# A three-stage kernel (linear attention, mixture of experts, SoLU layer): the last stage's blocks all behind the expert pairs

## The chip, the cores and the metric

One core of a Trainium2 chip runs the whole program in one launch. The metric is the device time of one execution in microseconds (us). Engines are named as in the profile: PE (TensorE, matmul), PEld (its weight loads), DVE (VectorE), ACT (ScalarE), POOL (GpSimd), SP (SyncE, which here only reads registers and issues DMAs).

## What is computed

The reference, cut to what matters (8 batches, 8 heads, 576 positions, so 4608 tokens of 512 numbers; 8 experts; inner width 1024):

```
proj = x @ w_phi ; proj -= max|proj| ; phi = [exp(proj), exp(-proj)]      # for q and k
num = phi(q) @ (phi(k)^T v) ; den = phi(q) @ sum phi(k) ; x = num / den
logits = x @ w_gate + modality_bias[modality] ; e = argmax ; gate = softmax(logits)[e]
y = gate * (relu(x @ w1[e]) @ w2[e])                                       # one expert per token
h = y @ w_in ; solu = h * softmax(h) ; out = (layernorm(solu) * g_ln) @ w_out
```

All matrix products that matter are done as three products of a high part and a low part (`mm3`, line 1071): high by high, high by low, low by high. So each operand has to be split first: ACT copies the high part (rounded), and DVE or POOL subtracts it from the source to get the low part.

## The kernel before

**Stage 1, attention and gating** (lines 194 to 732) scatters each token's row into a list per expert in DRAM (`xe`). On its heels DVE works out a small table (`slot_table`, lines 735 to 833): which expert, which rows and which output columns each "unit" of the next stage has. SP reads its registers from that table, and nothing of the next stage that depends on them can be loaded before.

**Stage 2, the experts** (`moe`, from line 955). Units 0 and 1 belong to the fullest expert, which is known early; their weights are loaded and split before the table is there. Units 2 to 17 are pairs (256 tokens), unit 18 is a single (128 tokens), then four minis of up to 32 tokens are done together in `quad` (line 1317). A unit is two products: `mm1` (line 1114) with four weight chunks, `mm2` (line 1169) with four more. `split_raw` (line 928) splits one chunk of 128x1024: high part on ACT, low part on DVE, or on POOL where line 933 says so: for unit 1 the chunks in `POOL_FIRST`, which is (1, 3); for units from `NOPOOL` = 13 on the chunks in `POOL_SPLIT`, also (3, 7). `used` (line 1063) is called as each chunk has been multiplied: it splits the chunk `LOOK` = 4 ahead, has SP reload the raw buffer for the next unit (for the minis after unit 18: `load_mini`), and advances the preparation `bg`.

**The preparation** (`weights`, lines 974 to 1021) loads, converts and splits the last stage's weights `win` and `wout` in 65 small steps, mostly on DVE. `NPREP` (line 1054) spreads them evenly over the chunks of the units before `START`.

**Stage 3, the last stage**, is done in 36 blocks of 128 tokens. `load_y` fetches two blocks' `y` from DRAM, `yT` splits it (ACT, then POOL), `a3` (line 1223) multiplies by `win` into `h` (24 matmuls) and runs a chain on DVE and ACT (maxima, exponent, scaling) that ends in the tile `ex`; `lnT` (line 1248) transposes `ex` on PE and splits it; `a4` (line 1262) multiplies by `wout` (24 matmuls) and POOL scatters the rows to the output. One call of `block` (line 1427) issues, in this order: `lnT(i)`, any postponed transposes of an expert unit (`run_mids`), `yT(i+2)`, the load for a later pair of blocks, `a3(i+1)`, `a4(i)`. The first call has only `yT(1)` and `a3(0)`.

**Where the blocks stand.** `unit` (line 1381) calls `gap` ahead of `mm1` and between `mm1` and `mm2`; from unit `START` = 14 on, `gap` runs a block. Ahead of unit `START` - 1 `load_y(0)` is issued, behind it `yT(0)`. In `quad`, one block follows each step. What blocks are then left run by themselves. The single unit keeps its hidden rows in `m.hr`: two Relu (line 1142) write it, and `tr_single` (line 1102), postponed with `run_mids`, transposes and splits it before `mm2`. The single's output is likewise copied off PSUM (`yr`, line 1157) and transposed later (line 1162).

**The order of the instructions.** Inside `manual_schedule` the engines named take their instructions in the order in which the program issues them; elsewhere a planner orders them by its own simulation. Units 2 to 12 (up to `NMAN`) are issued with PE, ACT, DVE, POOL and SP all in program order, units 13 to 18 with SP alone; `quad` with PE, and the blocks after it with all.

```
def units(u0, u1):
    for u in range(u0, u1):
        if u == START - 1: run(bg); load_y(0)
        unit(u)
        if u == START - 1: yT(0)
with tc.manual_schedule(engines=MANUAL): units(2, NMAN)
units(NMAN, NU)                                   # NU = 19
with tc.manual_schedule(engines=QMAN):
    for _ in quad(): block()
while state[0] < NT: block()
```

Of the kernel before, what the change touches and what calls it, by code (L numbers as in the profile page):

```python
# [25 lines left out]
NPAIR = 16  # L26
NSING = 1
# [20 lines left out]
RING = 5  # L48
RING0 = 1
STEP0 = 6  # L50
POOL_FIRST = (1, 3)
LOOK = 4
MANUAL = {mybir.EngineType.PE, mybir.EngineType.Activation, mybir.EngineType.DVE, mybir.EngineType.Pool}

# [805 lines left out]
class Moe:  # L860
# [67 lines left out]
    def split_raw(self, s, i):  # L928
# [3 lines left out]
        lo = pool.tile([P, DFF], F32R, name=nm[1])  # L932
        pe = POOL_FIRST if s == 1 and i < 4 else POOL_EARLY if s < NOPOOL else POOL_SPLIT
        self.split(self.raw[i], hi, lo, self.tc.nc.gpsimd if i in pe else self.tc.nc.vector)
# [20 lines left out]
def moe(ctx, m):  # L955
# [97 lines left out]
    NSTEP = 4 * (2 * KD + KF) + 2  # L1053
    NPREP = 8 * (START - 2) - 6

    def split_to(j):
        while done[0] <= min(j, len(order) - 1):
            ch = order[done[0]]
            done[0] += 1
            m.split_raw(*ch)  # L1060
            reload(*ch)

    def used(ch):
        split_to(pos[ch] + LOOK)
        if 2 <= ch[0] < START:
            uses[0] += 1
# [150 lines left out]
    def yT(i):  # L1217
        hi = p2.tile([P, KD, P], F32R, name="yTh")
        lo = p2.tile([P, KD, P], F32R, name="yTl")
        m.split(ys[i][0], hi, lo, G)  # L1220
        yt[i] = (hi, lo)
# [146 lines left out]
    def run(g):  # L1368
        for _ in g:
            pass  # L1370
# [10 lines left out]
    def unit(u):  # L1381
        gap(u)
        g = mm1(u)
        for i in range(4):
            next(g)
            if i == XAT:
                run_mids()
                next_x(u)
        run(g)
        gap(u)  # L1390
        run_mids()
        run(mm2([u]))
# [34 lines left out]
    def block():  # L1427
        i = state[0]
        state[0] += 1
        if 0 <= i < NT:  # L1430
            lnT(i)
        run_mids()
        if i + 2 < NT:
            yT(i + 2)
            if i % 2 and i + 3 < NT:
                load_y((i + 3) // 2)
        if i + 1 < NT:
            a3(i + 1)
        if 0 <= i < NT:
            a4(i)  # L1440

    def gap(u):
        if u >= START:
            block()

    def units(u0, u1):
        for u in range(u0, u1):
            if u == START - 1:
                run(bg)
                load_y(0)  # L1450
            unit(u)
            if u == START - 1:
                yT(0)

    with tc.manual_schedule(engines=MANUAL):
        units(2, NMAN)
    units(NMAN, NU)
    if ENDMAN:
# [7 lines left out]

XAT = 1
ENDMAN = True
START = 14
NMAN = START - 1  # L1470
QMAN = {mybir.EngineType.PE}
NOPOOL = 13


POOL_SPLIT = (3, 7)
# [57 lines left out]
```

## Time and profile before

| | before |
|---|---|
| median of 3 runs | 1337.44 us (1335.55 to 1338.93) |
| the profiled execution's own time | 1330.52 us |
| its span (first to last instruction) | 1328.8 us |
| mean granted clock of PE | 0.995 |
| busy: PE, PEld, DVE, ACT, POOL | 98%, 82%, 61%, 50%, 33% of the span |
| DMA | 120 MB by the queues, mean 90 GB/s |

Busy time is a share of the whole span; it says nothing of which engine the end waits for at a given moment. That is read from the waits and from the chain that ended last. PE's clock is given as a share of full speed (1.00 is 2.4 GHz, 0.50 is 1.2 GHz); a stretch with a value between spent part of it at either.

### The profile page before, as it was taken

The numbers are of one execution on the slowest core, as the hardware profiler recorded it, in microseconds if no ns is written. First come the engines' busy times: TensorE is split into PE (matmuls) and PEld (weight loads), VectorE is DVE, ScalarE is ACT, GpSimd is POOL, SyncE is SP. The second block draws the span as 40 slices with busy tenths as digits, with TensorE's granted clock in tenths as the row PEclk, the third lists the DMA queues.
The fourth block names the chain that finished last, engine by engine and source line by source line (L and its number), as shares of the span: only waits on it lengthen the run. The fifth ranks groups of instructions, "written<-read, shape, count | busy, mean of one in ns | idle before, by whom it ended". The sixth has DMA issues, their size and how long they took to land.

```text
span 1328.8 us, 25500 instructions
## 1 busy us (share of the span) xinstructions
PE 1298.4 (98%) x9522; PEld 1092.2 (82%) x9522; DVE 811.5 (61%) x1571; ACT 668.1 (50%) x1254; POOL 433.8 (33%) x493
## 2 busy tenths in 40 slices
PE   8999999999999989999999999999999999999997
PEld 7677777777775889999999999898987777888885
DVE  8758867866885748888888654444433334444442
ACT  6666666666664345555565554444433333443332
POOL 7555665674672200000000322232312232322331
PEclk9999999999999989999999999999999999999998
DMA  8712421341142132224432211124435542111110
GB/s 239 208 52 63 133 94 56 98 136 49 50 134 76 67 95 80 74 71 142 145 80 81 65 41 56 41 61 146 127 81 159 159 145 70 49 40 48 40 41 24
DMA packets 123119, 120.08 MB, mean 90 GB/s; under 512 B 35664, under 2 KB 109552, under 8 KB 122992
## 3 DMA queue, kind: packets, MB, share of 16 engines
q1 hardware_dynamic: 117008, 99.30, 25.6%
q0 software_dynamic: 5824, 19.04, 3.9%
q8 instruction: 77, 1.26, 0.4%
q14 instruction: 50, 0.41, 0.1%
q10 hardware_dynamic: 160, 0.07, 0.0%
HBM read 148.32 MB, written 33.02 MB: 136 GB/s over the span
## 4 chain that ended last, share of the span: by engine, by line
PE 63%; issue 1%; ACT 0%; POOL 0%; POOLq 0%
PE tp L1074 43%; PE h L1074 15%; PE tp L1098 2%; PE tp L898 1%; PE tp L1349 1%; PE tp L1333 1%; PE tp L1280 0%; POOLq L1529 0%; ACT sq L1253 0%; ACT lnTh L887 0%; PE tp L1109 0%; ACT wab L1268 0%; POOL rs L1258 0%; PE tp L1162 0%; POOL rs L1256 0%
## 5 line engine op out<-in xcount | busy, mean ns | idle before, releaser
L322 POOL TENSOR_TENSOR es<-es,e 128x512 f32<-128x512 f32 x128 | 163.6, 1285 | 103.9 <-ACT e L278 92.3
L1074 PE MATMUL tp<-xTh,whi 128*128 128x256 f32 x432 | 122.5, 284 | 2.9 <-PEq L1412 2.9
L1233 DVE TENSOR_REDUCE s_mx<-h 128x1 f32<-128x512 f32 x72 | 46.4, 686 | 125.4 <-PE h L1074 125.4
L1074 PE MATMUL tp<-xTh,wlo 128*128 128x256 f32 x432 | 121.5, 281 | 1.2 <-DVE wlo L926 1.2
L1074 PE MATMUL tp<-xTl,whi 128*128 128x256 f32 x432 | 121.3, 281 | 0.0
L1074 PE MATMUL tp<-hTl,whi 128*128 128x256 f32 x432 | 120.9, 280 | 0.0
L1074 PE MATMUL tp<-hTh,wlo 128*128 128x256 f32 x432 | 120.8, 280 | 0.0
L1074 PE MATMUL tp<-hTh,whi 128*128 128x256 f32 x432 | 120.7, 280 | 0.0
L926 POOL TENSOR_TENSOR wlo<-ldk,whi 128x1024 fp32r<-128x1024 f32 x6 | 14.6, 2435 | 314.8 <-PE tp L1074 296.0
L1269 POOL DMA_INDIRECT out_dram<-wab,gt x36 | 38.5, 1070 | 222.5 <-ACT wab L1268 221.8
L1238 ACT ACTIVATE ex<-h,s_mx,gt 128x1024 f32<-128x1024 f32 x36 | 43.4, 1206 | 134.2 <-DVE s_mx L1235 70.6
L271 DVE TENSOR_REDUCE m<-mm 128x4 f32<-128x512 f32 x144 | 97.1, 680 | 16.0 <-PE mm L269 15.9
L259 DVE TENSOR_TENSOR lo<-tp,hi 128x512 fp32r<-128x512 f32 x72 | 49.5, 688 | 84.0 <-ACT hi L258 83.5
L267 PE MATMUL mm<-wphi_hi,hi 128*128 128x256 f32 x288 | 93.5, 325 | 1.0 <-ACT hi L258 1.0
L1074 PEld LDWEIGHTS tp<-xTh,whi 128*128 128x128 f32 x432 | 82.0, 190 | 3.3 <-issue 3.1
L888 DVE TENSOR_TENSOR lnTl<-tp,lnTh 128x512 fp32r<-128x512 f32 x74 | 47.6, 685 | 58.4 <-ACT lnTh L887 58.4
L1074 PEld LDWEIGHTS tp<-xTh,wlo 128*128 128x128 f32 x432 | 82.0, 190 | 1.5 <-DVE wlo L926 1.5
L338 ACT ACTIVATE qp<-tp 128x512 f32<-128x512 f32 x128 | 69.4, 597 | 26.1 <-PE tp L330 23.2
L1074 PEld LDWEIGHTS tp<-xTl,whi 128*128 128x128 f32 x432 | 82.0, 190 | 0.2
L1074 PEld LDWEIGHTS tp<-hTh,whi 128*128 128x128 f32 x432 | 81.5, 189 | 0.4
L1074 PEld LDWEIGHTS tp<-hTl,whi 128*128 128x128 f32 x432 | 81.5, 189 | 0.3 <-DVE hTl L1089 0.2
L1074 PEld LDWEIGHTS tp<-hTh,wlo 128*128 128x128 f32 x432 | 81.5, 189 | 0.2
(427 smaller groups left out, 3928.2 us busy)
## 6 DMA issues: line engine op xcount, KB each, us to landing
ldk<-in_moe_w_dram SPq DMA_DIRECT2D x66, 512.0 KB
ldv<-in_moe_w_dram SPq DMA_DIRECT2D x66, 512.0 KB
ldq<-in_moe_w_dram SPq DMA_DIRECT2D x44, 512.0 KB
yd<-yo SPq DMA_DIRECT2D x36, 256.0 KB
yin<-yd SPq DMA_DIRECT2D x18, 512.0 KB
xin<-xe SPq DMA_DIRECT2D x16, 512.0 KB
ldk<-in_k_dram SPq DMA_DIRECT2D x15, 512.0 KB
ldq<-in_q_dram SPq DMA_DIRECT2D x15, 512.0 KB
```

The costliest lines, as they stand in the source:

```text
L259: V.tensor_tensor(out=lo, in0=tp, in1=hi.bitcast(F32), op=ALU.subtract)
L267: T.matmul(o, lhsT=hi[:, 2 * a + j, :], rhs=c.wphi_hi, start=(j == 0), stop=False, skip_group_check=True)
L271: V.tensor_reduce(out=m, in_=pj, axis=AX.X, op=ALU.max, apply_absolute_value=True)
L322: G.tensor_tensor(out=eo, in0=eo, in1=ev[:, :, r, :], op=ALU.add)
L338: A.activation(u.qp[half][:, fh, 2 * hp : 2 * hp + 2, o : o + 2 * P], tp.rearrange("p (h r) t -> p h (r t)", r=2), AF.Exp, scale=sc,)
L888: self.tc.nc.vector.tensor_tensor(out=lo, in0=tp, in1=hi.bitcast(F32), op=ALU.subtract)
L926: eng.tensor_tensor(out=lo, in0=src, in1=hi.bitcast(F32), op=ALU.subtract)
L1074: T.matmul(o, lhsT=l, rhs=r, start=first and n == 0, stop=last and n == 2, skip_group_check=True)
L1098: T.transpose(tp[:, j, :], src[:, (b0 + j) * P : (b0 + j + 1) * P], c.ident)
L1233: V.tensor_reduce(out=mx, in_=h[:, sl], axis=AX.X, op=ALU.max, negate=True)
L1238: A.activation(ex, h, AF.Exp, bias=mx, scale=g, accum_out=sm)
L1269: ins = G.indirect_dma_start(out=out, out_offset=bass.IndirectOffsetOnAxis(ap=ys.pop(i)[2].bitcast(I32), axis=0), in_=ob, in_offset=None,)
```

## The change

Five constants change, nothing else. `START` becomes 2 + 16 + 1 = 19, one behind the last unit. So `gap` never runs a block; `load_y(0)` moves from ahead of unit 13 to ahead of unit 18 and `yT(0)` from behind unit 13 to behind unit 18; the ten blocks that ran in units 14 to 18 join those in and behind `quad`. The preparation is spread over the chunks of units 2 to 18 instead of 2 to 13 (`NPREP` is 130 instead of 90). `NMAN` becomes 19: units 13 to 18 are now issued in program order on all engines. `POOL_FIRST` is empty and `NOPOOL` is 19, so no low part of an expert weight is on POOL any more: 2 of unit 1 and 12 of units 13 to 18 move to DVE.

```diff
-POOL_FIRST = (1, 3)
+POOL_FIRST = ()
...
-START = 14
-NMAN = START - 1
+START = 2 + NPAIR + NSING
+NMAN = START
 QMAN = {mybir.EngineType.PE}
-NOPOOL = 13
+NOPOOL = START
```

## Rows read from the trace of the kernel before

**Rows 1.** The profile's page: busy time, share of the span and instructions of each engine.

```profile
PE 1298.4 (98%) x9522; PEld 1092.2 (82%) x9522; DVE 811.5 (61%) x1571; ACT 668.1 (50%) x1254; POOL 433.8 (33%) x493
```

**Rows 2.** Busy time by stretch: length, engines (instructions), PE clock, DMA share, GB/s.

```profile
438.00:478.00 40.00, 32.59 (x259) 31.94 (x259) 27.68 (x98) 15.83 (x22) 5.74 (x3) 0.96 0.13 37
478.00:743.00 265.00, 265.00 (x2251) 264.84 (x2250) 218.55 (x298) 143.09 (x196) 2.63 (x1) 0.99 0.33 96
743.00:993.00 250.00, 250.00 (x1643) 227.01 (x1642) 115.90 (x183) 113.15 (x170) 72.46 (x72) 1.00 0.27 79
993.00:1131.00 138.00, 138.00 (x831) 106.56 (x830) 52.86 (x110) 48.37 (x86) 36.77 (x60) 1.00 0.41 130
1131.00:1309.50 178.50, 178.50 (x833) 145.43 (x831) 76.85 (x159) 67.92 (x121) 53.95 (x89) 1.00 0.14 42
```

**Rows 3.** The chain that ended last: start us, us, engine, tile, line, count.

```profile
696.92 22.49 PE tp L1074 x192
...
743.72 16.88 PE tp L1074 x144
...
1288.04 0.87 PE tp L1098 x8
1288.91 5.59 PE h L1074 x24
```

**Rows 4.** PE's waits from 438 us to the end: total us, times, longest.

```profile
PE tp L898 <- DMA xin<-xe: 3.0, 1, 3.0
PE tp L1074 <- PEq L1412: 2.9, 1, 2.9
PE tp L1074 <- DVE wlo L926: 1.2, 1, 1.2
```

**Rows 5.** Timeline around the table: start us, us, engine, line [idle before].

```profile
438.47 5.47 DVE L751 TENSOR_TENSOR st_tail<-st_tail,st_mini 128x8 f32<-128x8 f32 x1
...
439.12 2.44 POOL L926 TENSOR_TENSOR wlo<-ldq,whi 128x1024 fp32r<-128x1024 f32 x1
...
441.50 2.40 POOL L926 TENSOR_TENSOR wlo<-ldk,whi 128x1024 fp32r<-128x1024 f32 x1
...
444.00 0.15 DVE L751 TENSOR_TENSOR st_num<-st_all,st_tail 128x8 f32<-128x8 f32 x1
...
459.70 0.17 DVE L832 CAST st_tab<-st_res 128x5 int32<-128x5 f32 x1
...
462.46 0.39 SPq L913 DMA_DIRECT2D xin<-xe  x1
...
467.60 1.06 PE L898 MATMUL tp<-ident,xin 128*128 128x128 f32 x8 [2.96 <-DMA xin<-xe]
```

**Rows 6.** Busy time by stretch behind PE's three waits, columns as in the second group.

```profile
446.00:465.00 19.00, 18.43 (x154) 18.22 (x154) 13.70 (x75) 3.38 (x5) 0.00 (x0) 1.00 0.07 18
465.00:472.00 7.00, 4.40 (x25) 4.43 (x26) 4.18 (x5) 4.98 (x7) 0.00 (x0) 0.76 0.10 30
...
478.00:485.00 7.00, 7.00 (x49) 7.00 (x48) 0.69 (x1) 1.36 (x2) 0.00 (x0) 0.76 0.71 143
```

**Rows 7.** Groups by form, 478 to 1000 us (POOL: 743 to 1310): busy us, mean ns.

```profile
L1142 ACT ACTIVATE ldq<-tp 128x512 f32<-128x512 f32 x2 | 1.2, 592 | 0.1
L925 ACT CAST whi<-ldk 128x1024 fp32r<-128x1024 f32 x40 | 42.4, 1060 | 16.0 <-PE tp L1074 9.5 <-issue 4.0 <-DMA ldq<-in_moe_w_dram 1.7
L925 ACT CAST yTh<-yin 128x512 fp32r<-128x512 f32 x13 | 8.0, 623 | 40.6 <-DMA yin<-yd 28.7 <-PE h L1074 11.8
...
L926 DVE TENSOR_TENSOR wlo<-ldk,whi 128x1024 fp32r<-128x1024 f32 x35 | 43.6, 1246 | 12.6 <-ACT whi L925 12.3
L888 DVE TENSOR_TENSOR xTl<-tp,xTh 128x512 fp32r<-128x512 f32 x31 | 20.0, 685 | 17.0 <-ACT xTh L887 17.0
...
L926 POOL TENSOR_TENSOR yTl<-yin,yTh 128x512 fp32r<-128x512 f32 x36 | 47.4, 1318 | 65.8 <-ACT yTh L925 65.8
```

**Rows 8.** DVE timeline of one late block: first and last step of its chain.

```profile
1294.54 1.29 DVE L1233 TENSOR_REDUCE s_mx<-h 128x1 f32<-128x512 f32 x2 [3.93 <-PE h L1074]
...
1299.21 0.88 DVE L1245 TENSOR_SCALAR ex<-ex,s_tot 128x512 f32<-128x512 f32 x2
```

## The prediction

> **What bounds the kernel now.** I read the page first, then the busy time by stretch, the chain that ended last, PE's waits, and last the timeline where those waits are. The page says PE is busy for 98% of the span [rows 1]; the stretches say where the rest is not. From 478 to 1309.5 us PE is busy for every microsecond, in the pairs alone, in the pairs mixed with blocks, in the minis and in the blocks alone [rows 2]. The chain that ended last is PE from end to end there. Its pace tells whether a busy PE hides slack: 192 matmuls of a pair alone in 22.49 us are 117 ns each, 144 between blocks in 16.88 us also 117 ns, and 24 matmuls of a block, twice as wide, in 5.59 us are 233 ns [rows 3]. So a matmul costs the same wherever it stands, and moving ten blocks moves PE work without making it smaller. What can change is idle time of PE: three waits at the start of the experts, of 1.2, 3.0 and 2.9 us [rows 4], and any that the new order makes. DVE, ACT and POOL have room everywhere in these stretches [rows 2].
>
> **What goes away, at the front.** POOL's two low parts of unit 1 run from 439.12 to 443.90. Across both of them DVE is held in one tiny subtraction of the table for 5.47 us, though the like of it takes 0.15 [rows 5]: 5.3 us lost. From there DVE is busy without a pause up to the table's last step at 459.70, SP then issues the load of `xin` at 462.46, and PE stands 2.96 us until that has landed [rows 5]. With the change DVE does the two low parts itself, 2 x 1.25 = 2.5 us by the group of its low parts [rows 7], and is not held. The table, and all behind it, comes 5.3 - 2.5 = **2.8 us** earlier. PE's 1.2 us wait for a low part of POOL's [rows 4] goes, so PE reaches the transposes of `xin` 1.2 us earlier and waits about 1.4 us instead of 3.0; the sum is the same 2.8. The wait of 1.2 us left the clock at 1.00; after the waits of 3.0 and 2.9 us it was 0.76 over 7 us each time, which is 0.24 x 7 = 1.7 us lost per wait [rows 6]. I take it that the shortened wait no longer costs that: **1.7 us**. The wait at the branch (2.9, line 1412) stays: PE's own sequencer is what it waits for. Front: -4.5. Bounds: at best all of 1.2 + 3.0 + 1.7 = 5.9; at worst nothing, if the planner, which still orders the table, puts the two low parts ahead of more of it.
>
> The Trainium skill ("SBUF — State Buffer", "Who interferes with whom") has DVE with two SBUF inputs and a reading GpSimd instruction exclude each other, for the whole of the instruction that came first. The row agrees that DVE stands still, but it stood for two POOL instructions, not one; by the page's one, what goes would be 2.4 us, about as much as DVE takes on. That case is among the rivals.
>
> **What is moved at no cost.** Twelve low parts of units 13 to 18 come to DVE, 1.25 us each [rows 7], two per unit. In the pairs alone DVE already does all eight of a unit and the whole preparation in eleven units, 218.55 us of 265, and PE never waits [rows 2]; spread over sixteen units the preparation weighs less. If that cover were gone, PE would wait at a chunk, at most 1.25 us each. `load_y(0)` now stands in SP's queue between the last output writes of unit 17 and the chunk reloads and mini weights of unit 18, and waits for those writes as it did for unit 12's; a load of that size landed 5.1 us after issue [rows 5], and unit 18 takes 11 us. A moved block takes its loads, its split on POOL and its scatter along; the blocks alone need 53.95 us of POOL in 178.5 [rows 2].
>
> **What the new order adds.** PE now has nothing between the steps at the seam of experts and blocks. Three holes, priced by the rows of the pieces:
> - In unit 18 a block used to stand between `mm1` and `mm2`. Now, after the last matmul of `mm1`: Relu 0.59, the high part of the last chunk 1.06 (ahead on ACT in program order), its low part 1.25 on DVE, then the low part of the first hidden half 0.69: 3.6 us to the first matmul that needs it [rows 7]. PE fills 0.87 with eight transposes [rows 3] and 0.2 with two matmuls. Hole: **2.5**. Bounds 0.8 (Relu, copy and low part without the chunk) to 3.6 (nothing filled).
> - After unit 18 the single's rows are copied off PSUM, about 0.6 like the Relu, and transposed, 0.44; `yT(0)` behind it needs 0.62 on ACT and 1.3 on POOL [rows 7] before the third matmul of `a3(0)`. 0.6 + 0.62 + 1.3 and some 0.4 for starts are 2.9, of which PE fills 0.9. Hole: **2.0**, bounds 0.6 to 2.6.
> - The first block's chain: from the end of `h` to a whole `ex` it is 1294.54 to 1300.09, 5.55 us [rows 8]. In the steady run `a4` of the block before, 5.59 us [rows 3], just covers it. For block 0 there is no such `a4`, and in program order only the four transposes of the minis' input, 0.44 us, stand between; the transposes of `ex` can start some 0.3 before its end. Hole: **4.8**, bounds 4.8 to 5.2. Before, unit 14's `mm1` of 11 us filled it.
> - A hole longer than the 2.9 us that was followed by a 0.76 clock should cost 1.7 us again [rows 6]; the two shorter, broken holes I take like the 1.2 us that cost nothing. **1.7**, bounds 0 to 3.4.
>
> Seam: +11.0, bounds 6.2 to 14.8. **Sum:** -4.5 + 11.0 = +6.5 us. The profiled execution would go from 1328.8 to 1335.3 us of span, 1337.0 with the 1.7 around it. It lies 6.9 us under the median of the runs shown, so the sum is put on the median: 1337.4 + 6.5 = **1343.9 us**, slower by 0.5%. A measurement of this kernel can tell about 0.3%, 4.0 us, from no change. The ends give +0.3 to +14.8.
>
> **The rivals.**
> - Nearly even: the front gives its full 5.9 and the two short holes stay near their lower bounds. +0.3 to +4 us, some 1340. For it: both short holes are sums of single steps in program order, some of which may overlap. Against: the 4.8 alone nearly eats the 5.9.
> - Faster: the seam is covered, since PE's order is not as written (a planner that slips the single unit's or the minis' matmuls ahead of the waiting transposes). Then only the front is left, 1337.4 - 4.5 = 1332.9. It decides if under 0.5 us of holes is left. Against: the change puts PE in program order through units 13 to 18, `quad` and the blocks, and the late blocks of the chain come out exactly as issued [rows 3].
> - The lock is short: one POOL instruction's worth. The table comes no earlier, PE's 1.2 us only moves into the wait for `xin`, and the front gives nothing: 1337.4 + 11.0 = 1348.4. Against: 5.47 us in one row [rows 5]. The Trainium skill's page named above reads this way.
> - The queue at the seam: SP stands at `load_y(0)`, and behind it four mini weights and the minis' input are late, at the 130 GB/s of the mini stretch [rows 2]. The input may come 5 us late inside the 4.8 hole; beyond that PE waits for it: at 10 us late +5, 1348.8. Against: no PE wait for a DMA in that stretch now [rows 4].
>
> **How the numbers follow.** The forecast 0.52, nearly even 0.24, covered 0.07, the short lock 0.09, the queue 0.08. A little of the forecast's own spread falls under 4.0 us: slower 0.67, within 0.3% 0.26, faster 0.07. The range runs from even, 1337.5, to 1351.0, near the upper end of the sum; it leaves out the covered case and the last of the tails.
>
> **What would show it.** Right: the table's subtraction at about 0.15 us and its last step near 457; PE's wait for `xin` near 1 us and the clock at 1.00 behind it; two short PE waits around unit 18, and one near 5 us ahead of the first transposes of `ex`, with a low clock after it; PE's pace unchanged. Wrong: a seam without PE waits, new waits for weight chunks in units 13 to 18, or a front as before.

## The result, and the profile after

The kernel after takes **1344.17 us** (median of 6 runs, 1343.77 to 1344.55); the kernel before, run beside it, 1337.07 (6 runs). The ratio is 1.0053, 95% interval 1.0041 to 1.0065: slower by 7.1 us. The forecast was 1343.9 us and slower.

| | before | after |
|---|---|---|
| median of the runs | 1337.07 us | 1344.17 us |
| the profiled execution's own time | 1330.52 us | 1344.48 us |
| its span | 1328.8 us | 1342.7 us |
| mean granted clock of PE | 0.995 | 0.995 |

The two spans differ by 13.9 us, the medians by 7.1, so the spans can't be subtracted as they stand. First the page of after: PE has 3 us more busy time for the same 9522 matmuls, and POOL is 43 us down, most of it the fourteen low parts of 2.4 us [rows 1].

```profile
PE 1301.4 (97%) x9522; PEld 1093.2 (81%) x9522; DVE 816.0 (61%) x1585; ACT 665.9 (50%) x1254; POOL 391.2 (29%) x479
```

**The front.** The timeline around the table, after (start us, us, engine, line, [idle before]):

```profile
444.60 0.17 DVE L751 TENSOR_TENSOR st_tail<-st_tail,st_mini 128x8 f32<-128x8 f32 x1
...
462.68 0.17 DVE L832 CAST st_tab<-st_res 128x5 int32<-128x5 f32 x1
...
465.44 0.39 SPq L913 DMA_DIRECT2D xin<-xe  x1
...
470.79 1.07 PE L898 MATMUL tp<-ident,xin 128*128 128x128 f32 x8 [1.51 <-DMA xin<-xe]
```

The subtraction that took 5.47 us takes 0.17. It starts 6.1 us later than before (444.60 against 438.47), and what lies ahead of it is not touched by the change; the experiments show that this start moves by as much between profiles of kernels that are alike up to there. Counted from that subtraction, the table's last step comes after 18.08 us instead of 21.23, and PE's transposes of `xin` after 26.19 instead of 29.13 [rows 5]: 2.9 us earlier, with a wait of 1.5 instead of 3.0.

**PE's waits**, after, from 425 us to the end (total us, times, longest):

```profile
PE tp L1280 <- issue: 3.8, 1, 3.8
PE tp L1074 <- PEq L1412: 2.9, 1, 2.9
PE tp L898 <- DMA xin<-xe: 1.5, 1, 1.5
PE tp L1098 <- DVE ex L1245: 0.9, 1, 0.9
PE tp L1074 <- DVE hTl L888: 0.9, 1, 0.9
PE tp L1074 <- ACT hTh L887: 0.8, 1, 0.8
PE tp L1162 <- ACT yr L1157: 0.7, 1, 0.7
PE h L1074 <- POOL yTl L926: 0.6, 1, 0.6
PE tp L1109 <- ACT ldq L1142: 0.5, 1, 0.5
```

Against three waits before [rows 4], the wait for a low part is gone, that for `xin` is half, that at the branch is the same, and seven are new. All seven stand at the seam of experts and blocks. Their places in PE's timeline, after:

```profile
863.07 0.66 PE L1109 MATMUL tp<-ident,ldq 128*128 128x128 f32 x4 [0.50 <-ACT ldq L1142]
864.49 0.50 PE L1074 MATMUL tp<-w,hTh 128*128 128x256 f32 x2 [0.76 <-ACT hTh L887]
865.87 0.39 PE L1074 MATMUL tp<-w,hTl 128*128 128x256 f32 x1 [0.88 <-DVE hTl L888]
...
872.26 0.66 PE L1162 MATMUL tp<-ident,yr 128*128 128x128 f32 x4 [0.68 <-ACT yr L1157]
...
874.14 0.50 PE L1074 MATMUL h<-win0h,yTl 128*128 128x512 f32 x1 [0.63 <-POOL yTl L926]
...
883.32 0.63 PE L1280 MATMUL tp<-ident,xin 128*128 128x128 f32 x4 [3.78 <-issue]
884.83 1.94 PE L1098 MATMUL tp<-ident,ex 128*128 128x128 f32 x8 [0.89 <-DVE ex L1245]
```

The first three are the single unit between its two products, the next two its rows and the first `y`, the last two the first block's chain.

**The clock**, after, by stretch (length, engines, PE clock, DMA share, GB/s):

```profile
468.00:474.00 6.00, 4.49 (x39) 4.32 (x39) 3.21 (x3) 4.31 (x7) 0.00 (x0) 1.00 0.11 32
479.00:488.00 9.00, 8.56 (x50) 8.59 (x51) 0.69 (x1) 1.53 (x2) 0.00 (x0) 0.64 0.58 122
495.00:839.00 344.00, 344.00 (x2942) 344.00 (x2941) 262.80 (x343) 186.41 (x253) 0.00 (x0) 1.00 0.28 84
862.00:885.00 23.00, 14.89 (x91) 11.95 (x90) 8.31 (x14) 7.02 (x12) 2.57 (x2) 0.99 0.59 161
885.00:893.00 8.00, 8.00 (x33) 6.74 (x33) 1.46 (x3) 2.84 (x5) 2.66 (x5) 0.80 0.24 66
1025.00:1323.00 298.00, 298.00 (x1385) 242.66 (x1384) 129.74 (x269) 111.95 (x199) 90.38 (x149) 1.00 0.14 43
```

Behind the shorter wait for `xin` the clock stays at 1.00, where it was 0.76 [rows 6]. Behind the branch it is 0.64 over 9 us, 3.2 us lost, where before it lost 1.7; so in these two executions what the clock gained at `xin` it lost again behind the branch. In the pairs and in the blocks alone PE has no idle time, as before [rows 2].

**The sum by the chain that ended last.** Five pieces of it, after (the third is the product behind the last wait at the seam):

```profile
488.02 0.87 PE tp L898 x8
...
699.56 22.49 PE tp L1074 x192
...
886.77 6.29 PE h L1074 x24
...
1314.89 5.59 PE h L1074 x24
...
1323.45 2.71 issue
```

and the two of before that answer to the first and the last of these:

```profile
485.14 0.87 PE tp L898 x8
...
1309.55 2.71 issue
```

PE's pace is the same to the hundredth [rows 3]. Three landmarks split the 13.9 us: the table's subtraction, the transposes in unit 2, and the last block's end. Up to the subtraction, after is 6.1 us late (444.60 against 438.47), which is not the change's doing. From there to the transposes of unit 2 it gains 3.25 (43.42 instead of 46.67). From those to the last block it loses **11.0** (835.43 instead of 824.41). From the last block to the end both take 19.25. So the change is worth -3.25 + 11.0 = +7.8 us in these two executions; the medians say 7.1.

### The profile page after: what moved, and what is told of

Same layout as the page of the kernel before. It is cut to its first block, busy times and chain, and to the rows that moved or that the text cites. A ratio compares the mean times of both kernels' runs of the same rounds, so it can differ in the third digit from the quotient of the medians.

```text
span 1342.7 us, 25519 instructions
## 1 busy us (share of the span) xinstructions
PE 1301.4 (97%) x9522; PEld 1093.2 (81%) x9522; DVE 816.0 (61%) x1585; ACT 665.9 (50%) x1254; POOL 391.2 (29%) x479
## 4 chain that ended last, share of the span: by engine, by line
PE 62%; issue 1%; DVE 0%; DMA 0%; ACT 0%; POOL 0%; POOLq 0%; DVEq 0%
PE tp L1074 42%; PE h L1074 15%; PE tp L1098 2%; PE tp L898 1%; PE tp L1349 1%; PE tp L1333 1%; DMA ldk<-in_moe_w_dram 0%; DVE wlo L926 0%; POOLq L1529 0%; PE tp L1280 0%; ACT ex L1238 0%; DVE ex L1243 0%; POOL yTl L926 0%; ACT sq L1253 0%; ACT lnTh L887 0%
## 5 line engine op out<-in xcount | busy, mean ns | idle before, releaser
L926 POOL TENSOR_TENSOR yTl<-yin,yTh 128x512 fp32r<-128x512 f32 x36 | 46.4, 1288 | 429.3 <-ACT yTh L925 429.3
L268 PE MATMUL mm<-wphi_lo,hi 128*128 128x256 f32 x288 | 81.2, 282 | 0.0
```

Source lines behind the costliest of these rows:

```text
L268: T.matmul(o, lhsT=hi[:, 2 * a + j, :], rhs=c.wphi_lo, start=False, stop=False, skip_group_check=True)
L926: eng.tensor_tensor(out=lo, in0=src, in1=hi.bitcast(F32), op=ALU.subtract)
```

## Experiments

Theory: the change is two things that have nothing to do with each other. At the front, DVE is no longer held by POOL (a gain); at the seam, PE has three holes that a block used to fill, and the clock behind them (a loss). Rivals: the front gains nothing by itself, or the loss is spread over program order, more low parts on DVE and later preparation. The runs below were made on three chips, and the kernel before has a median of its own on each: 1335.1 us (the kernel before once more, the two low parts alone, the two on POOL again, and one block back), 1328.42 (the four experiments behind "that last wait") and 1335.32 ("that last wait"). So each time stands beside before's on the same chip, and kernels of different chips are compared by ratio.

**The kernel before once more.** No edit.

> The kernel before, unchanged, profiled once more. In the two profiles shown, the experts' first matmul stands at 438.8 us before and at 445.0 us after, although nothing was changed ahead of it but where two low parts run. If those 6 us are a difference between executions, this profile may have the experts' start anywhere between 438 and 446 us, and its time will follow it. If the change itself delays the attention stage, this one starts at 438.8 us again, within 1 us.

It took 1334.34 us (one run). Its row of the held subtraction, by tile (all line numbers are one higher here): duration in ns, then the start:

```profile
L752 DVE TENSOR_TENSOR st_tail<-st_tail,st_mini x1: 5454/5454/5454, 442.9 to 442.9; 128x8 f32<-128x8 f32 x1
```

The same program reaches this point at 442.9 us here and at 438.5 in the profile shown, and its span is longer by 3.8 us. The later profiles say what this goes with: the four of this chip have the start of this subtraction at 442.9 to 445.5 us, the four of the second chip at 436.9 to 438.0, and on both chips there are kernels with the two low parts on POOL and without. So it is mostly the chip, and not the change; which chip the two profiles shown come from is not known. Only stretches counted from a common landmark can be compared between profiles, or medians of runs on one chip.

**The two low parts alone.**

```diff
 # on the kernel before
-POOL_FIRST = (1, 3)
+POOL_FIRST = ()
```

> The kernel before with the two low parts of unit 1 on DVE and nothing else changed; blocks, preparation and the order of units 13 to 18 as before. Theory (the front and the seam are two separate things; the front is the held DVE): about 3 us faster than before, 1334, ratio 0.9975 or so; the table's subtraction at 0.15 us; the wait for the experts' input near 1.5 us and none for a low part. Rival (the front gains nothing by itself, as the branch behind it absorbs it or as the clock comes back later): 1337, ratio 1.000.

Measured: 1331.54 against 1335.1 us of before, ratio **0.9977** (0.9968 to 0.9986). PE's waits in it, at the front:

```profile
PE tp L1074 <- PEq L1412: 2.6, 1, 2.6
PE tp L898 <- DMA xin<-xe: 1.8, 1, 1.8
```

No wait for a low part, 1.8 us for `xin`, the subtraction at 0.17 us. The front is worth 3.1 us by the ratio (3.6 by the medians) by itself, and this version beats both kernels. The rival, 1.000, lies outside the interval. The profiles agree: from the start of the held subtraction to the start of unit 3 it is 68.8 to 70.1 us in the four with both low parts on POOL and 65.2 to 66.9 in the six with none, 3.4 us between the means.

**After, with the two low parts on POOL again.**

```diff
 # on the kernel after
-POOL_FIRST = ()
+POOL_FIRST = (1, 3)
```

> The kernel after, but with the two low parts of unit 1 on POOL again. Theory: the front's 3 us come back, about 1347.3 us, ratio to before 1.0078; the table's subtraction takes over 5 us again and the seam is as in the kernel after. Rival (the front gains nothing): 1344.2, ratio 1.0053.

Measured: 1346.67 us (5 runs, 1345.09 to 1350.99), ratio 1.0092 (1.0075 to 1.011). The expected 1.0078 is inside the interval, near its lower end, and the rival's 1.0053 is outside. The held subtraction is back at 5.46 us. The profiled execution is longer than the median, and shows why single executions spread: the waits at the seam add up to 8.4 us, hardly more than in after, but the clock fell in more places there (columns as in the second group of rows):

```profile
860.00:870.00 10.00, 7.86 (x59) 7.18 (x58) 7.89 (x8) 7.77 (x11) 0.00 (x0) 0.90 0.81 246
870.00:880.00 10.00, 8.71 (x49) 7.97 (x49) 0.00 (x0) 2.21 (x4) 1.56 (x2) 0.75 0.69 224
880.00:890.00 10.00, 5.54 (x26) 4.25 (x25) 3.35 (x8) 1.77 (x3) 0.99 (x1) 0.93 0.25 41
890.00:900.00 10.00, 9.60 (x36) 8.06 (x37) 2.62 (x5) 2.73 (x5) 2.61 (x5) 0.73 0.19 53
```

That is 1.0 + 2.5 + 0.7 + 2.7 = 6.9 us at the lower clock, but not all of it is time lost: some falls where PE stood waiting for `ex` anyway (0.62 from 888.0 to 890.4 us). In the table at the end of this section the stretch is 3.8 us longer than in after, with 0.3 us more of waits, so the clock cost some 3.5 us more than the 1.8 of after (an estimate from these two lengths). What a hole costs in clock is not one number.

**One block back into the experts.** The first block call goes between the two products of unit 18; `load_y(0)` and `yT(0)` move up by a unit. The edit, cut:

```diff
 # on the kernel after, in unit() and units()
         run(g)
+        if u == NU - 1:
+            block()
         gap(u)
...
-            if u == START - 1:
-                run(bg)
-                load_y(0)
+            if u == START - 2:
+                load_y(0)
+            if u == START - 1:
+                run(bg)
             unit(u)
-            if u == START - 1:
+            if u == START - 2:
                 yT(0)
```

> The kernel after, but the first block call (the split of the second y and the first product with win) stands between the two products of unit 18, and the load and the split of the first y one unit earlier. Everything else as after: preparation over all units, program order, no low part on POOL. Theory (the loss is three holes at the seam and the clock behind them): nearly all of the 11 us comes back, since that product of 5.6 us covers the single unit's steps and the second product of unit 18 covers the block's chain; about 1333.5 us, ratio 0.997, below the kernel before by the front's 3 us. Rival (the loss is spread: program order in units 13 to 18, twelve low parts more on DVE, later preparation): at most half comes back, 1339 or more.

Measured: 1332.93 us beside 1335.1, ratio **0.9985** (0.9976 to 0.9994). PE's waits from the front on:

```profile
PE tp L1074 <- PEq L1414: 3.6, 1, 3.6
PE tp L1109 <- ACT ldq L1142: 1.0, 1, 1.0
PE tp L898 <- DMA xin<-xe: 0.7, 1, 0.7
```

Six of the seven waits at the seam are gone with the move of a single block of 36 and of its load; the one left is for the single's second Relu, 1.0 us, which stands on ACT behind the high parts of two chunks. Against after (1.0053) 0.0068 comes back, some 9 us, and the kernel is faster than before although preparation, program order and low parts stay as the change put them. The spread-out rival, which wanted 1339 or more, falls. It remains 0.0008 above the two low parts alone; the intervals overlap, and the 1.0 us wait would be as much. The table at the end of this section says that it is: between unit 3 and the last block's end this kernel loses 0.9 us against before, with a wait of 1.0 us. That leaves late blocks, the spread preparation and program order no more than a few tenths of a us.

**That last wait.** On top of the edit above, the second half of the single's rows is transposed behind the block's product, not ahead of it.

```diff
 # in unit(), on the edit above; tr_single becomes two steps, the second kept in late
         if u == NU - 1:
             block()
+            late.pop()()
```

> The kernel with one block back in unit 18, and the second half of the single unit's hidden rows transposed behind that block's product instead of ahead of it. Theory (the only hole left at the seam is PE's 1.0 us wait for the second Relu, and nothing else separates that kernel from the one with the two low parts alone): about 1 us faster than the kernel with one block back, ratio 0.9978, the same as the two low parts alone (0.9977), and no PE wait over 0.3 us between the pairs and the minis. Rival (late blocks, the spread preparation or hand order in units 13 to 18 cost about 1 us by themselves): ratio 0.9985 as before that edit.

Measured: 1335.25 beside 1335.32, ratio 1.0000 (0.9991 to 1.0009). A miss of the forecast, 0.9978: the edit moved the wait. The timeline of PE in it:

```profile
869.96 0.39 PE L1074 MATMUL tp<-whi,hTh 128*128 128x256 f32 x1 [0.16 <-ACT hTh L887]
...
871.81 1.06 PE L1098 MATMUL tp<-ident,ex 128*128 128x128 f32 x8 [1.34 <-DVE ex L1246]
...
876.26 0.66 PE L1163 MATMUL tp<-ident,yr 128*128 128x128 f32 x4 [0.68 <-ACT yr L1158]
```

The low part of that half now stands in DVE's queue behind the block's whole chain, so `mm2` lacks it; the transposes of `ex`, issued later by the program, stand in the middle of `mm2` (so program order does not hold across the boundary of two hand-ordered regions), and they wait too. That makes 2.2 us at the seam in place of 1.0. Another 1.3 us of waits for DVE stand in unit 2, and the edit does not reach there: the chain goes through a load of a piece of `win` of 5.25 us for the preparation, which DVE's low parts of that unit then stand behind. Such waits in unit 2 also came in two other kernels (0.6 us with the twelve low parts alone, 0.7 in after with them on POOL) and in none of the other profiles. Theory and rival both lie outside the interval, so these runs do not settle whether late blocks cost anything by themselves; the length of the kernel with one block back does, in the table at the end of this section.

**The twelve late low parts on DVE, alone.**

```diff
 # on the kernel before
-NOPOOL = 13
+NOPOOL = 19
```

> The kernel before with the twelve low parts of units 13 to 18 on DVE and nothing else changed. Theory (DVE has room there, PE waits for no chunk): no difference, ratio 0.999 to 1.001. Rival (the low parts on DVE are part of the loss): slower by 2 us or more, with PE waits for low parts between 743 and 993 us.

Measured: 1328.4 beside 1328.42, ratio 1.0001 (0.9992 to 1.001). From 743 to 993 us PE stays busy throughout and DVE goes from 115.90 [rows 2] to 127.19 us. In the table at the end of this section its length is that of before. These low parts are no part of the loss while the blocks stand among the units.

**After, with the twelve low parts on POOL.**

```diff
 # on the kernel after
-NOPOOL = START
+NOPOOL = 13
```

> The kernel after with the twelve low parts of units 13 to 18 on POOL again. Theory (no cost and no gain in the pairs; in unit 18 the last chunk's low part no longer stands ahead of the hidden rows' low part on DVE): as after or up to 1 us faster, ratio 1.004 to 1.006, the wait for the hidden rows' low part (0.9 us) smaller. Rival (POOL's low parts were worth something in the pairs): faster by 2 us or more, ratio 1.0035 or less, with waits for low parts in after that are gone here.

Measured: 1337.23 beside 1328.42, ratio 1.0064 (1.005 to 1.0078), overlapping the interval of after. The wait for the hidden rows' low part did shrink, from 0.9 to 0.2 us, but another came, in the first product of unit 18 (at 853.51 us):

```profile
PE tp L1074 <- POOL wlo L926: 1.0, 1, 1.0
```

One more of 0.7 us, for a low part on DVE, is in unit 2 (at 491.83 us), where the two kernels do not differ; it comes with the load of `win` told of above. In a single unit a product lasts 5.6 us, and POOL takes 2.4 us for a chunk, which came too late here. Before, a block stood around it. The runs do not tell this kernel from after; in the profiles the stretch of the table is 0.9 us longer here, about the wait for POOL.

**After, with units 13 to 18 ordered by the planner.**

```diff
 # on the kernel after
-NMAN = START
+NMAN = 13
```

> The kernel after, but units 13 to 18 ordered by the planner on PE, ACT, DVE and POOL, as before. Theory (the holes come from what is there to do, not from writing the order by hand): no block is in these units, so the planner has nothing to fill with; the three holes stay within 1 us, ratio 1.004 to 1.007. Rival (the covered case: the planner slips the first block's product or the single unit's steps between): most of the 11 us comes back, ratio 0.997 to 1.000.

Measured: 1335.02 beside 1328.42, ratio 1.0045 (1.0029 to 1.006). PE's waits at the seam (cut):

```profile
PE tp L1280 <- issue: 3.1, 1, 3.1
PE tp L1098 <- DVE ex L1245: 1.5, 1, 1.5
...
PE tp L1162 <- ACT yr L1157: 0.7, 1, 0.7
...
PE tp L1109 <- ACT ldq L1142: 0.3, 1, 0.3
PE tp L1074 <- DVE hTl L888: 0.2, 1, 0.2
```

The planner shortens the hole in unit 18 from 2.1 to 0.5 us, more than the 1 us allowed for, and hides the split of the first `y`; the large hole ahead of the first block stays at 4.6. In the table the stretch is 3 us shorter than in after; by the runs the two cannot be told apart. The covered rival, 0.997 to 1.000, is out: the large hole had nothing to cover it.

**One low part on POOL instead of two.**

```diff
 # on the kernel after
-POOL_FIRST = ()
+POOL_FIRST = (1,)
```

> The kernel after with one of the two low parts of unit 1 on POOL (chunk 1), the other on DVE: how long one POOL instruction holds DVE. Theory (DVE stands while POOL's subtractions run, however many follow each other): the table's subtraction takes about 3.0 us instead of 5.5 and 0.17, that is one instruction of 2.4 and the 0.6 by which it was issued earlier. Rival (DVE is held by something else than the length of POOL's work): 5.5 or 0.17 us.

It took 1338.93 us (one run, so no ratio). DVE's and POOL's timeline in it:

```profile
436.94 3.13 DVE L751 TENSOR_TENSOR st_tail<-st_tail,st_mini 128x8 f32<-128x8 f32 x1
```

```profile
437.60 2.44 POOL L926 TENSOR_TENSOR wlo<-ldq,whi 128x1024 fp32r<-128x1024 f32 x1
```

With no low part on POOL the subtraction takes 0.17 us, with one 3.13, with two 5.47 [rows 5]; it ends each time within 0.04 us of POOL's last one. So DVE is held for one instruction of POOL at a time, and for the next as well where POOL follows on at once, 2.3 us more. The rule of the Trainium skill ("SBUF — State Buffer", "Who interferes with whom") is that of two such instructions the one that issues first has the ports for its whole length and the other blocks. These rows agree that the one left waiting stands for the whole of a POOL instruction. They do not agree on which one waits: by its record DVE's subtraction starts 0.66 us ahead of POOL's here. Nor is a second POOL instruction that goes ahead of the waiting one in that rule; the rows show it.

**One stretch in all profiles.** From the transposes at the start of unit 3 (`tp`, line 898, the piece of the chain behind those of unit 2) to the last block's end, in us, each read from the chain that ended last as above; what stands behind it takes 19.2 to 19.3 in each:

| kernel | from | to | length | against before |
|---|---|---|---|---|
| before | 508.58 | 1309.55 | 800.97 | |
| before once more | 512.47 | 1313.39 | 800.92 | -0.05 |
| the two low parts alone | 508.88 | 1309.81 | 800.93 | -0.04 |
| the twelve late low parts on DVE, alone | 507.45 | 1308.37 | 800.92 | -0.05 |
| one block back into the experts | 510.06 | 1311.95 | 801.89 | +0.9 |
| that last wait | 509.79 | 1313.50 | 803.71 | +2.7 |
| after, units 13 to 18 ordered by the planner | 504.60 | 1313.54 | 808.94 | +8.0 |
| after | 511.45 | 1323.45 | 812.00 | +11.0 |
| after, the twelve low parts on POOL | 503.16 | 1316.09 | 812.93 | +12.0 |
| after, one low part on POOL | 504.17 | 1317.90 | 813.73 | +12.8 |
| after, the two low parts on POOL again | 514.29 | 1330.05 | 815.76 | +14.8 |

The stretch holds the seam and nothing of the front. The four kernels that keep ten blocks in units 14 to 18 agree within 0.05 us, and every kernel without a block there is slower by 8 us or more.

## Why the prediction was right

**PE's work is conserved.** Right: 22.49 us for 192 matmuls and 5.59 for 24 in both kernels, and no idle time in pairs or blocks (from 495 to 839 us and from 1025 to 1323 us in after).

**The front, -4.5.** The 2.8 us of the held DVE were 2.9 at PE's transposes: that term was right in mechanism and in size. The 1.7 us of clock behind the wait for `xin` was saved there as assumed (1.00 in place of 0.76), but the low clock behind the branch, costed as unchanged, took 3.2 us instead of 1.7, so that in this execution next to nothing of the clock term was left. With the two low parts alone the clock behind the branch was 0.86 over 10 us, 1.4 lost: this loss varies between executions. So it was -3.25 in that execution, and -3.1 by the runs of the two low parts alone: mis-sized by some 1.3 us, in the clock, not in the held DVE. The rival of the short lock is out by those runs, and its premise by the three lengths 0.17, 3.13 and 5.47 us of the subtraction. The nearly even case is out as well, since it needed 5.9 us here and both short holes near their lower bounds.

**The seam, +11.0.** By the chain +11.0. The three holes were costed at 2.5, 2.0 and 4.8. PE's listed waits are 2.1 (0.50 + 0.76 + 0.88), 1.3 (0.68 + 0.63) and 4.7 (3.78 + 0.89), 8.1 together. A listed wait is shorter than what it costs, since the last matmul ahead of it is drawn at its full 0.28 us while the next would have started after 0.117. Counted from start to start, less the pace of the matmuls ahead, the holes are 2.8, 1.6 and 5.0, 9.4 together, where 9.3 was put. The clock cost 1.8, where 1.7 was put: the eight transposes of `ex` took 1.94 in place of 0.87 [rows 3], and the product behind them 6.29 in place of 5.59. Unit 3 took 0.2 less than before (23.43 us from its transposes to the next ones, 23.66 before). 9.4 + 1.8 - 0.2 = 11.0.

That the sum meets 11.0 to the tenth is partly luck. The hole of unit 18 was larger than forecast and the second one smaller, and in two other kernels with the same seam the stretch from unit 3 to the last block's end cost 12.8 and 14.8 us (the table). There the clock fell already behind the waits of 0.5 to 0.9 us in unit 18, to 0.79 from 856 to 864 us with one low part on POOL, and to 0.57 from 868 to 876 us with two. The prediction took such short, broken holes to cost no clock; that was so in after (1.00 from 864 to 872 us), and not in these.

**The queue at the seam.** The minis' input was late, as the rival had it, but without its price and for the most part not for its reason. PE stood 3.8 us ahead of the transposes of the minis' input, and 0.9 for `ex` after it. SP issued the last of the four loads only at 878.81:

```profile
869.67 0.43 SPq L1323 DMA_DIRECT2D xin<-xe  x1
...
875.94 0.43 SPq L1323 DMA_DIRECT2D xin<-xe  x1
...
878.81 0.44 SPq L1323 DMA_DIRECT2D xin<-xe  x1
```

What held SP between them was not `load_y(0)`, where it stood 2.3 us (the other wait on that line, 4.6, is for a later pair of blocks), but the small writes of the gate rows `gd` (line 922), one behind each of these loads, which wait for one another. Such waits stood there before as well, 6.1 us, with blocks for PE to do meanwhile. SP's waits of this kind from 860 to 890 us, after (total us, times, longest):

```profile
SPq L922 <- DMA gd<-xe: 8.0, 3, 4.9
```

The first block's chain ran underneath, as the prediction said of an input up to 5 us late. Where the input came sooner the two waits add up to much the same: 1.8 and 2.9 us with one low part on POOL, and none and 4.9 with two. (The time given with this rival, 1348.8, should read 1348.9, which is 1343.9 + 5.)

**The moved low parts and the preparation at no cost.** Right: ratio 1.0001 for the twelve low parts alone, and a kernel with all of it ran at 0.9985 once one block was back, with 0.9 us lost behind unit 3 and a wait of 1.0 us to account for it.

**The total.** +6.5 was forecast, +7.1 measured. In the aligned profiles (+7.8) the 1.3 us too much at the front are the whole of what the forecast missed. By the runs both halves were put too large and the errors partly cancel: the front gave 3.1 instead of 4.5, and the seam took some 10 instead of 11.0 (1.0053 against 0.9977 of the two low parts alone).

## What to carry to other kernels

Where one engine is busy to the microsecond, moving its work is worth nothing and costs whatever stood between two dependent steps: at each seam of two stages ask what fills the first item's chain, and leave one item of the next stage there (one block of 36 was worth 9 us here). And a small instruction on the way to a table or an address is the wrong one to run beside work on an engine that can hold it: the two low parts that looked free on the idle POOL cost 3 us by delaying a subtraction of 0.17 us.

## What the runs showed of the hardware that was not expected

- Nearly the same waits cost different amounts of clock in different executions: behind 8.1 us of listed waits at the seam the clock cost 1.8 us in one, and behind 8.4 us some 5.3 in another (the 1.8 and the 3.5 more from above).
- DVE's held subtraction starts 0.65 us ahead of the POOL instruction that holds it (438.47 and 439.12 [rows 5]; 436.94 and 437.60), although at its start only an indirect DMA is on POOL; in the kernel after it runs in 0.17 us beside such a DMA. Whether POOL's record starts late or something of that DMA counts was not tried.
- Up to the experts' table, profiles of kernels that are alike up to there, but for where two low parts run, differ by up to 8.6 us (436.9 to 445.5). Four profiles on one chip lie within 2.6 us and four on another within 1.1.
